# A fused retention and channel-mixing kernel: the order of the first loads, and the operand of the zero products

## The chip, the cores and the metric

The kernel runs on one core of one Trainium2 chip. The metric is the device time of one execution in microseconds (us), given as the median of several runs. A separate execution is taken by the hardware profiler; its span runs from the first to the last instruction on the core.

The engines are named as in the profile: PE is the matrix engine (TensorE; PEld its weight loads, which overlap with its products), DVE is VectorE, ACT is ScalarE, POOL is GpSimd, and SP is the engine that only issues transfers. ACT can issue transfers too. A trailing q (SPq, ACTq) stands for an issue.

## The reference

Two stages. The first is a retention layer over 4 batches, 8 heads, 768 positions and 64 channels, in blocks of 64 positions with a state that decays by head. The second is a channel-mixing layer on its output. Cut to what matters:

```python
# retention, for each block of 64 positions
intra = einsum('bhic,bhjc->bhij', qb, kb) * Dmask        # Dmask: powers of lam[h]
out   = einsum('bhij,bhjd->bhid', intra, vb) + einsum('bhid,bhde->bhie', qb * lam_pow, kv_state)
kv_state = lam_block * kv_state + einsum('bhsd,bhse->bhde', kb * rev_pow, vb)

# channel mixing on x, the output with all heads side by side (512 channels)
xk = mu_k * x + (1 - mu_k) * x_prev                      # x_prev: x one position earlier
xr = mu_r * x + (1 - mu_r) * x_prev
k  = maximum(xk @ w_k, 0)                                # 512 -> 1024
y  = sigmoid(xr @ w_r) * (k * k @ w_v)
```

## The kernel before

The positions are cut into six tiles of 128 (two blocks of 64 each), the heads into four pairs. Each tile passes through scores, decay, values and states of the four pairs, then through mixing, and then through the three large products with w_r, w_k and w_v. Each of those is done in three passes over operands split into a high and a low part, on 128x512 tiles.

The order of all work is written out by hand in one long string, ORDER. Each token names a step and its indices. All engines follow program order in their own queues, and waits between engines are semaphores. The string begins with `Z10 L00 T0 L02 A00 T2 a00 k02 A02 B00 k00 Sk4 ...`.

What the change and the steps of the prediction touch, all in the first 30 us:

- `zeros` is a work tile that VectorE clears with a memset (line 146). It is viewed as bfloat16 and used by `keep_busy` (line 200). Z10 issues ten products on `zeros` into the unused PSUM tile `idle`; each has 128 stationary and 512 moving columns. They compute nothing that is read later.
- `smalls` (30 KB) holds the small constants: the decay factors and their helpers, mixing weights, masks. `eye` (64 KB) is a 128x128 identity. SP issued the first, ScalarE the second.
- From `smalls`, VectorE, ScalarE and POOL build powers of the decay factors (`pows`, `steps`, `PW`, `KD`) and the tile `rows`. T0 transposes `rows` on PE with `eye` into `table`, from which the decay table Dt is copied.
- `load_first` issues SP's loads of the first tile's q, k and v, `in`: two transfers of 1 MB for head pairs 0 and 2, and two pairs of 768 and 256 KB for head pairs 1 and 3. In between, `stage_part` issues the halves of w_k, w_r and w_v (`raw`).
- Each weight half is converted once: `conv_top` casts part of its bits (`top`; for the blocks Sk4 to Sk7 on POOL, which waits for the half's landing alone), `conv_bits` puts the rest beside it (`raw`), `conv_split` makes the high and low parts (`wk`).
- `mix_prev` and `mix` make the mixed inputs (`ts`). POOL copies the last column of each (`lastw`), and `split_x` makes `xh` and `xl`.

Hardware transfers take eight semaphore counters in turn, in an order that the scheduler sets. A transfer that takes a counter again waits on the issuing engine until the transfer that had it before has landed.

Of the kernel before, what the change touches and what calls it, by code (L numbers as in the profile page):

```python
# [7 lines left out]
F32 = mybir.dt.float32  # L8
# [28 lines left out]
def tile_retention_moe(  # L37
# [25 lines left out]
    tensor, vector, scalar, gpsimd, sync = (  # L63
        InOrder(tc, e) for e in (tc.nc.tensor, tc.nc.vector, tc.nc.scalar, tc.nc.gpsimd, tc.nc.sync))
# [3 lines left out]
    work = ctx.enter_context(tc.tile_pool(name="work", bufs=2))  # L68
# [60 lines left out]
            sync.dma_start(t[rows, e:e + 2].rearrange("p c o -> p (c o)"), qv[n - 1, hp, rows])  # L129

    smalls = tiny.tile([128, 52 + H], F32, name="smalls")
    sync.dma_start(smalls, small)
    eye = work.tile([128, 128], F32, tag="rt", name="eye", bufs=4)
    scalar.dma_start(eye, hot)
    lows, impulse, ecol, lrow, erow, prow, mus, pair, parity = (smalls[:, a:b] for a, b in (
# [6 lines left out]
    KD = tiny.tile([128, H], F32, name="KD")  # L142
    one = tiny.tile([128, 1], F32, name="one")
    gpsimd.memset(one, 0.0)
    zeros = work.tile([128, 512], F32, tag="kf", name="zeros")
    vector.memset(zeros, 0.0)
    vector.memset(steps8[:, 0:8], 0.0)
    tops = const.tile([128, 2, 1024, 2], U16, tag="top", name="top")
# [30 lines left out]
    idle = ps_m.tile([128, 512], F32, tag="m", name="idle")  # L179
# [18 lines left out]
    zeros = zeros.bitcast(mybir.dt.bfloat16)  # L198

    def keep_busy(count):  # L200

        for _ in range(count):
            tensor.matmul(idle, zeros[:, 0:128], zeros[:, 512:1024], start=True, stop=True)

    def split(hi, lo, x):
        scalar.copy(hi, x)
# [285 lines left out]
    for step in ORDER.split():  # L492
        if step[0] == "T":
            powers(step)
        elif step[0] == "Z":
            keep_busy(int(step[1:]))
        else:
            i, j = step[1], int(step[2])
            steps[step[0]](i if i in "rkv" else int(i), j)
# [91 lines left out]
```

## Time and profile before

| | before |
|---|---|
| median of 3 runs | 398.38 us (397.89 to 399.62) |
| profiled execution, whole | 398.97 us |
| its span | 397.2 us |
| PE busy | 389.0 us, 98% |
| DVE busy | 245.5 us, 62% |
| ACT busy | 201.7 us, 51% |
| POOL busy | 39.8 us, 10% |
| bytes moved | 42.58 MB |

The span is the profiled execution less what lies around it, 1.77 us. Products are pipelined and their ends are modelled, so a product's length in a row is more than the distance to the next one. The granted clock is a share of 2.4 GHz. Transfers have two times: that of the issue (a row with SPq or ACTq) and the one from issue to landing. Queue q1 holds what SP issued, q10 what ScalarE issued; a packet is one row of a transfer, or the small write that reports an engine's share as done.

### The profile page before, as it was taken

Reading aid. Unit: us, or ns where it says so; the run is one execution under the profiler, and the core shown is the slowest. Engines: PE = TensorE matmul, PEld = TensorE weight load, DVE = VectorE, ACT = ScalarE, POOL = GpSimd, SP = SyncE. Lnnn points to the kernel's source line nnn. Section 1 sums busy time; section 2 is a strip of 40 time slices with the busy share of each in tenths; the row PEclk is TensorE's granted clock in tenths of the full one; section 3 lists DMA queues with packets and bytes.
Section 4 is the critical chain, followed back from the end, with each engine's and each line's share of the span. In section 5 each row is a group of like instructions: output and inputs, shape, how many; then the busy total and the mean of one; then the engine's idle time right before and its main releaser. Section 6 shows DMA issues by size and latency. Waiting matters only on the chain.

```text
span 397.2 us, 8411 instructions
## 1 busy us (share of the span) xinstructions
PE 389.0 (98%) x3532; PEld 321.3 (81%) x3532; DVE 245.5 (62%) x392; ACT 201.7 (51%) x367; POOL 39.8 (10%) x104
## 2 busy tenths in 40 slices
PE   7989999999999999999999999999999999999996
PEld 4758887888888888888888888888888888888886
DVE  5797899789865465876656365865546844222411
ACT  4889998565866172365721456731266542132400
POOL 5375000110110010000100010120000000000000
PEclk9999999999999999999999999999999999999999
DMA  7998735566060073170621070250100001000002
GB/s 275 417 356 276 295 125 174 169 150 216 11 205 0 10 218 94 28 186 0 184 57 54 28 194 20 82 159 26 53 2 2 2 1 55 26 26 2 0 34 73
DMA packets 12886, 42.58 MB, mean 107 GB/s; under 512 B 1840, under 2 KB 2224, under 8 KB 12592
## 3 DMA queue, kind: packets, MB, share of 16 engines
q1 hardware_dynamic: 9104, 35.68, 28.3%
q10 hardware_dynamic: 3744, 6.36, 4.4%
q8 instruction: 28, 0.46, 0.5%
q14 instruction: 10, 0.08, 0.1%
HBM read 35.74 MB, written 6.29 MB: 106 GB/s over the span
## 4 chain that ended last, share of the span: by engine, by line
PE 92%; DVE 2%; issue 1%; POOL 0%; ACT 0%; POOLq 0%
PE vp L33 33%; PE kp L33 31%; PE rp L33 17%; PE xp L33 5%; PE sc L33 3%; PE u L33 3%; DVE xl L33 1%; DVE raw L33 0%; DVE wk L33 0%; DVE ts L33 0%; POOL top L33 0%; POOL lastw L33 0%; DVE rt L33 0%; ACT st L33 0%; POOL ts L33 0%
## 5 line engine op out<-in xcount | busy, mean ns | idle before, releaser
L33 PE MATMUL vp<-wv,k 128*128 128x512 f32 (+1 forms) x600 | 134.7, 382 | 0.0
L33 PEld LDWEIGHTS vp<-wv,k 128*128 128x128 f32 x600 | 108.8, 188 | 22.2 <-DVE wv L33 0.3
L33 PE MATMUL kp<-xh,wk 128*128 128x512 f32 x384 | 123.1, 391 | 0.0
L33 PEld LDWEIGHTS kp<-xh,wk 128*128 128x128 f32 x384 | 72.0, 188 | 15.7 <-DVE wk L33 0.5
L33 PE MATMUL kp<-xl,wk 128*128 128x512 f32 x192 | 74.9, 390 | 0.1
L33 PE MATMUL rp<-wr,xh 128*128 128x512 f32 x192 | 59.5, 391 | 0.0
L33 DVE TENSOR_TENSOR kf<-kf 128x512 f32<-128x512 f32 x40 | 27.3, 691 | 51.6 <-ACT kf L33 51.4
L33 ACT ACTIVATE kf<-kp 128x512 f32<-128x512 f32 x48 | 28.2, 595 | 54.6 <-PE kp L33 38.1
L33 DVE TENSOR_TENSOR xl<-ts,xh 128x512 fp32r<-128x512 f32 x48 | 33.3, 699 | 21.7 <-ACT xh L33 21.6
L33 ACT COPY qv<-st 64x256 f32<-64x256 f32 x80 | 32.4, 405 | 27.3 <-DVE st L33 23.3
L33 ACT CAST xh<-ts 128x512 fp32r<-128x512 f32 x48 | 29.4, 617 | 29.5 <-DVE rt L33 22.9
L33 PEld LDWEIGHTS kp<-xl,wk 128*128 128x128 f32 x192 | 36.0, 188 | 8.1 <-DVE xl L33 0.7
L33 PEld LDWEIGHTS rp<-wr,xh 128*128 128x128 f32 x192 | 35.8, 188 | 7.6
L33 DVE TENSOR_TENSOR rt<-vp,rt 128x512 f32<-128x512 f32 (+1 forms) x25 | 16.4, 666 | 38.4 <-PE vp L33 38.4
L33 PE MATMUL rp<-wr,xl 128*128 128x512 f32 x96 | 37.4, 390 | 0.0
L33 ACT ACTIVATE ts<-xp,omu 128x512 f32<-128x512 f32 x40 | 26.2, 688 | 17.5 <-PE xp L33 16.1
L33 DVE TENSOR_TENSOR mv<-qv,LP 64x256 f32<-64x256 f32 x80 | 33.6, 420 | 1.5
L33 DVE TENSOR_TENSOR mv<-sc,Dt 64x512 f32<-64x512 f32 (+1 forms) x48 | 32.6, 685 | 2.3 <-ACT in L33 1.4
L33 DVE SCALAR_TENSOR_TENSOR ts<-xp,smalls,ts 128x512 f32<-128x512 f32 x40 | 29.2, 746 | 7.4 <-ACT ts L33 7.1
L33 DVE TENSOR_TENSOR k<-kf,k 128x1024 fp32r<-128x1024 f32 x24 | 29.3, 1224 | 7.0 <-ACT k L33 6.7
L33 POOL COPY ts<-lastw 128x4 f32<-128x4 f32 x48 | 18.0, 378 | 134.9 <-DVE xl L33 134.9
L33 ACT ACTIVATE rt<-rp 128x512 f32<-128x512 f32 x24 | 13.9, 592 | 30.7 <-PE rp L33 30.7
(66 smaller groups left out, 299.0 us busy)
## 6 DMA issues: line engine op xcount, KB each, us to landing
qv<-qv SPq DMA_DIRECT2D x40, 256.0 KB, 6.3
kin<-kk SPq DMA_DIRECT2D x20, 512.0 KB, 5.3
out<-rt ACTq DMA_DIRECT2D x23, 256.0 KB, 2.0
raw<-w_v SPq DMA_DIRECT2D x4, 1023.8 KB, 6.8
in<-qvk SPq DMA_DIRECT2D x2, 1024.0 KB, 6.1
raw<-w_k SPq DMA_DIRECT2D x2, 1023.8 KB, 13.0
raw<-w_k SPq DMA_DIRECT2D x4, 511.8 KB, 12.7
raw<-w_r SPq DMA_DIRECT2D x4, 511.8 KB, 15.2
```

The lines of the kernel that those rows point to most:

```text
L33: return lambda *args, **kw: self.tc.keep_in_program_order(op(*args, **kw))
```

## The change

Three edits. The load of `smalls` is issued by ScalarE, ahead of that of `eye`, and no longer by SP. The tile `zeros` has 64 words per partition in place of 512, so the memset is shorter. The zero products take these 64 words (128 bfloat16 values) as the stationary operand and, read four times over through a dimension of step zero, as the moving one. There are ten products before and after, each with 512 moving columns.

```diff
     smalls = tiny.tile([128, 52 + H], F32, name="smalls")
-    sync.dma_start(smalls, small)
+    scalar.dma_start(smalls, small)
     eye = work.tile([128, 128], F32, tag="rt", name="eye", bufs=4)
     scalar.dma_start(eye, hot)
...
-    zeros = work.tile([128, 512], F32, tag="kf", name="zeros")
+    zeros = work.tile([128, 64], F32, tag="kf", name="zeros")
     vector.memset(zeros, 0.0)
...
-            tensor.matmul(idle, zeros[:, 0:128], zeros[:, 512:1024], start=True, stop=True)
+            tensor.matmul(idle.rearrange("p (o x) -> p o x", o=4), zeros, zeros.rearrange("p (o x) -> p o x", o=1).broadcast_to([128, 4, 128]), start=True, stop=True)
```

SP's queue from its start, before. DMAHW0 to DMAHW7 are the eight counters; a number behind a name tells tiles of one name apart (`in_152` and `in_166` are head pairs 0 and 2, `in_214` and `in_216` pairs 1 and 3).

```order
L33 DMA smalls_103<-small 128x60
L33 DMA in_152<-qvk0 128x2048
L33 DMA in_166<-qvk0 128x2048
L33 DMA raw_206<-w_k 128x2047
L33 DMA in_214<-qvk0 128x1536
L33 DMA in_216<-qvk0 128x1536
L33 DMA in_214<-qvk0 128x512
L33 DMA in_216<-qvk0 128x512 [waits DMAHW0_49]
L33 DMA raw_206<-w_k 128x2047 [waits DMAHW1_49]
L33 DMA raw_276<-w_k 128x2047 [waits DMAHW2_49]
L33 DMA raw_276<-w_k 128x2047 [waits DMAHW3_49]
```

The same queue in the changed kernel.

```order
L33 DMA in_152<-qvk0 128x2048
L33 DMA in_166<-qvk0 128x2048
L33 DMA raw_206<-w_k 128x2047
L33 DMA in_214<-qvk0 128x1536
L33 DMA in_216<-qvk0 128x1536
L33 DMA in_214<-qvk0 128x512
L33 DMA in_216<-qvk0 128x512 [waits DMAHW0_49]
L33 DMA raw_206<-w_k 128x2047 [waits DMAHW1_49]
L33 DMA raw_276<-w_k 128x2047 [waits DMAHW2_49]
L33 DMA raw_276<-w_k 128x2047 [waits DMAHW3_49]
```

Every load of SP moves up by one place. The waits read alike, but other transfers have the counters: before, DMAHW0 to 3 were those of `eye`, `smalls`, `in_152` and `in_166`; now they are those of `smalls`, `in_152`, `in_166` and `eye`. From DMAHW4 on nothing differs.

ScalarE's queue from its start, before.

```order
L33 DMA eye_105<-hot 128x128
L33 ACT_TABLE_LOAD
L33 ACTIVATE one_111<-one_111 128x1 [waits Pool_49]
L33 ACTIVATE smalls_103<-smalls_103,pows_107 128x2 [waits DMAHW1_49,DVE_49]
L33 ACTIVATE smalls_103<-smalls_103,pows_107 128x4 [waits DVE_49,Activation_49]
```

And in the changed kernel.

```order
L33 DMA smalls_103<-small 128x60
L33 DMA eye_105<-hot 128x128
L33 ACT_TABLE_LOAD
L33 ACTIVATE one_111<-one_111 128x1 [waits Pool_49]
L33 ACTIVATE smalls_103<-smalls_103,pows_107 128x2 [waits DMAHW0_49,DVE_49]
L33 ACTIVATE smalls_103<-smalls_103,pows_107 128x4 [waits DVE_49,Activation_49]
```

One issue stands ahead of `eye`, of the activation table's load and of the small activations. PE's and POOL's orders are unchanged, and VectorE's too but for the size of its first memset.

## Rows read from the trace of the kernel before

**Rows 1.** The page: one engine's busy time; the last chain's shares by engine.

```profile
PE 389.0 (98%) x3532; PEld 321.3 (81%) x3532; DVE 245.5 (62%) x392; ACT 201.7 (51%) x367; POOL 39.8 (10%) x104
...
PE 92%; DVE 2%; issue 1%; POOL 0%; ACT 0%; POOLq 0%
```

**Rows 2.** Table of stretches: start:end, length, busy PE, PEld, DVE, ACT, POOL, clock, DMA.

```profile
5.70:9.40 3.70, 2.85 (x27) 2.18 (x26) 2.38 (x5) 1.46 (x5) 1.34 (x4) 1.00 1.01 363
30.00:390.00 360.00, 359.73 (x3258) 299.83 (x3258) 220.83 (x347) 180.14 (x328) 23.37 (x75) 1.00 0.28 88
```

**Rows 3.** Timeline, 0 to 6 us: start, length, engine, operation, [idle before, releaser].

```profile
0.73 0.42 ACTq L33 DMA_DIRECT2D eye<-hot  x1
...
0.73 0.38 SPq L33 DMA_DIRECT2D smalls<-small  x1
...
0.91 0.48 DVE L33 MEMSET zeros<- 128x512 f32 x1 [0.91 <-PEq L583]
1.17 0.90 SPq L33 DMA_DIRECT2D in<-qvk  x2
1.18 1.28 ACT L33 ACT_TABLE_LOAD   x1 [1.18 <-PEq L583]
1.35 0.07 DVE L33 MEMSET steps<- 128x8 f32 x1
...
1.45 4.45 PE L33 MATMUL idle<-zeros 128*128 128x512 bf16 x10 [1.45 <-DVE zeros L33]
...
2.65 0.63 ACT L33 ACTIVATE smalls<-smalls,pows 128x2 f32<-128x2 f32 x2
...
4.28 0.30 DVE L33 TENSOR_TENSOR rows<-smalls 128x136 f32<-128x136 f32 x1
...
5.69 1.13 PE L33 MATMUL table<-eye,rows 128*128 128x128 f32 x8
```

**Rows 4.** Issues in 0.7 to 2.31 and at 4.8 us: count, size, us to landing.

```profile
eye<-hot ACTq DMA_DIRECT2D x1, 64.0 KB, 1.9
smalls<-small SPq DMA_DIRECT2D x1, 30.0 KB, 1.7
...
raw<-w_k SPq DMA_DIRECT2D x1, 511.8 KB, 13.5
```

**Rows 5.** Chain of waits that ends at 40 us: start, length, piece.

```profile
18.34 0.77 POOL top L33
...
19.28 0.61 POOL lastw L33
...
29.79 10.31 PE kp L33 x44
```

**Rows 6.** Timeline, 4 to 20 us: the five w_k issues, one activation.

```profile
4.80 8.05 SPq L33 DMA_DIRECT2D raw<-w_k  x5
...
18.19 0.72 ACT L33 ACTIVATE ts<-raw,omu 128x512 f32<-128x512 f32 x1
```

**Rows 7.** Transfers in 4 to 6 us, all engines.

```profile
DMA packets 118, 0.84 MB, mean 418 GB/s; under 512 B 16, under 2 KB 16, under 8 KB 16
```

**Rows 8.** Transfer rate in 2.3 to 6.2 us, in 40 slices of 0.0975 us.

```profile
GB/s 84 84 252 84 168 0 84 84 168 504 420 420 420 420 420 504 420 420 504 252 420 504 336 336 420 588 252 336 588 420 336 504 336 420 504 336 336 420 420 252
```

**Rows 9.** Outputs issued at 141.94 and 152.14; packets by queue in 143.21 to 146.31.

```profile
out<-rt ACTq DMA_DIRECT2D x1, 256.0 KB, 4.9
...
out<-rt ACTq DMA_DIRECT2D x1, 256.0 KB, 2.1
...
q1 hardware_dynamic: 175, 0.56, 67.6%
q10 hardware_dynamic: 144, 0.26, 23.5%
```

**Rows 10.** Groups: DVE with a repeated operand (0 to 12 us), and without.

```profile
L33 DVE TENSOR_TENSOR mv<-sc,Dt 128x512 f32<-128x512 f32 x4 | 2.6, 686 | 1.9 <-ACT in L33 1.4 <-ACT Dt L33 0.5
...
L33 DVE TENSOR_TENSOR kf<-kf 128x512 f32<-128x512 f32 x40 | 27.3, 691 | 51.6 <-ACT kf L33 51.4
```

## The prediction, made before the changed kernel ran

> **What bounds the kernel now.** I read the page's shares first. TensorE is busy 98% of the span, and the chain that ended last is 92% PE [rows 1]. The table of stretches then says where PE is not busy: between 30 and 390 us it works 359.73 of 360 us [rows 2], so nothing in that stretch can be gained, and a stage before it is worth what it shifts the start of that unbroken run. All the change touches lies in the first 6 us. The question is how much earlier or later the run from 29.79 us starts.
>
> Two paths lead there.
>
> *The stream of loads.* The chain of waits goes back from 29.79 through conversions to POOL's cast `top` of the w_k half block at 18.34 [rows 5]. That cast waits for nothing but the block's landing. The DMA was issued at 4.80 and landed 13.5 us later, at 18.30 [rows 4, 6]. Its own 512 KB need 524 KB/418 GB/s = 1.25 us at the rate of the stretch 4 to 6 us [rows 7]; most of the rest it was queued behind earlier loads. So this landing moves with the start of the stream and not with its own issue.
>
> *The head.* The zero products start at 1.45, when the memset has ended at 0.91 + 0.48 = 1.39, and the table's transposes start at 5.69 behind them [rows 3]. The ten take 4.24 us, 0.424 each. Everything up to ScalarE's `ts` at 18.19 to 18.91 follows from there; POOL's `lastw`, which wants it, starts at 19.28 behind the cast [rows 5, 6]. So the head has 19.28 - 18.91 = 0.37 us of slack against the loads.
>
> **The change part by part.**
>
> *The memset.* 512 words took 0.48, the 8 of `steps` 0.07 [rows 3]. In a straight line between them 64 words take 0.07 + 0.41 x 56/504 = 0.12, so the zero products can start 0.36 us earlier, at 1.09, and end at 5.33 if each still takes 0.424. Without the fixed part (0.48 x 64/512 = 0.06) it would be 0.42.
>
> *The products that read 128 values four times.* Ten in number, as before, with as many columns. No row has a TensorE product whose moving operand repeats. The nearest are VectorE's: `mv<-sc,Dt`, which reads one head's table four times over, takes 686 ns for 512 columns, and the plain `kf<-kf` 691 [rows 10]. So repetition cost nothing there, and I put it at nothing here. A gain I exclude, as the same 512 columns pass; the other bound is twice the time, 4.24 us (below).
>
> *The first inputs at the head of SP's queue.* SP issued `smalls` at 0.73 and the first `in` at 1.17 [rows 3]; without the former the whole stream is issued 0.44 us earlier. What it loses: 30 and 64 KB of `smalls` and `eye` [rows 4] moved before the big rows had got going. The rate in 2.3 to 6.2 us stays under 260 GB/s for its first nine slices of 0.0975 us, up to 3.2 us, and is about 420 from there [rows 8]. If these 94 KB now fall into the full stream, they take 96 KB/418 GB/s = 0.23 us of it. So the stream moves by -0.44 to -0.21. I take -0.3, about the middle.
>
> *SP's waits.* A DMA waits for the one that last used its counter (the order in the section on the change). The second half of w_k's first block now waits for the first `in` rather than `smalls`: issued at about 5.8 instead of 4.80. The block behind it waits for the second `in`, and the next for `eye`. All of it is hidden: before the change that half landed 13.5 us after its issue, nearly all of it queueing, so one microsecond less of queueing is no later landing. If the queue ran dry it would cost that 1.0 us.
>
> *ScalarE.* One more issue before the activation table's load, 0.38 us: the load moves from 1.18 to 1.56 and ends at 2.84; the two small activations at 2.65 [rows 3] move to about 3.1 and end at 3.7. VectorE's `rows` at 4.28 wants them: hidden, with 0.6 us left.
>
> *The small transfers among the big rows.* `smalls` is issued at 0.73 still and landed 1.7 us later; `eye` goes from 0.73 to about 1.13, and with its 1.9 us lands at 3.03 if undisturbed [rows 3, 4]. But both now share the 16 engines with `in`. What that does is seen late in the kernel. An output of 256 KB, 128 rows, landed 2.1 us after its issue when alone, and 4.9 beside SP's loads; in that stretch SP's queue moved 175 packets and ScalarE's 144 [rows 9]. So rows of the two queues went about one for one, and the 8 rows that each engine had cost 2.8 us. An 8 KB row of `in` takes about 16 x 2.0/(118 - 16) = 0.31 us of an engine [rows 7], eight of them 2.5.
>
> For `smalls` I take nothing: it took 1.7 us with its landing, and the big rows reached their full rate only 3.2 - 1.17 = 2.0 us after their issue [rows 3, 8], now at 2.7 us. The far bound is +2.5 to +2.8. `rows` ended at 4.58, which leaves 5.33 - 4.58 = 0.75 us for a delay of `smalls`. For `eye`, half way through when the stream fills up, I take somewhere between 0 and 2.8: it lands between 3.0 and 5.8. The transposes then start between 5.33 and 5.85, which against 5.69 is -0.36 to +0.16; less the slack of 0.37 the head is ahead of the loads either way.
>
> The Trainium skill's page "DMA: Bandwidth & Descriptors", section "Issuing engines are not separate DMA queues", says that transfers of the different issuers run on the same 16 engines and interleave, and that a second issuer only saves the sequencer's time to start them. The trace agrees as to the mixing (175 and 144 packets in one stretch). By the page the whole gain is the saved issue, and the sum would be -0.44; by the row of the disturbed output the small transfers pay for it as well.
>
> **The sum.** Loads -0.3, head at most +0.16 - 0.37 = -0.21: the later of the two counts, between -0.2 and -0.3; I take -0.3. The profiled execution took 398.97 us (span 397.2), which becomes 398.7. It lies 0.6 above the median 398.38 of the runs shown, so that I forecast 398.1.
>
> **The rivals.**
>
> *Both small transfers are caught (slower).* If `smalls` has big rows before it on every engine, its 8 rows and then `eye`'s 8 go through one for one: 16 x 0.31 = 5.0 us on top of 3.03, so `eye` lands at 8.0 (2 x 2.8 by the output's row: 8.6). The transposes start 2.3 to 2.9 us later than 5.69; less 0.37 of slack the end comes 1.9 to 2.5 later: 400.3 to 400.9. It decides from a start of the transposes later than 5.69 + 0.37 = 6.06; below that it costs nothing. For it: the one-for-one mixing in [rows 9]. Against it: the 2.0 us that `in` needed to get going.
>
> *The stream does not start earlier*, because not SP's issue but the first rows themselves hold it up. The slow first slices in [rows 8] speak for it. Then the loads stay, the head hides behind them, and the time is 398.4.
>
> *The repeated operand is read more slowly.* At twice the time the zero products end at 1.09 + 8.48 = 9.57; +3.9 at the transposes, less 0.37: 401.9. For it speaks only that no row shows such a product; [rows 10] speak against.
>
> *TensorE's clock rises later.* The zero products take 0.424 us for 512 columns, the pace of 1.2 GHz, the lower of its two levels; for 5.7 to 9.4 us the granted clock is 1.00, 2.4 GHz [rows 2, 3]. If the zero products end early and PE then waits for `eye`, the rise could come after that stretch. Its 2.85 us of PE work [rows 2] would take twice that: +2.85 - 0.37 = +2.5, 400.9. Against it: the wait in my forecast is 0.5 us at most, behind 4.2 us of products. The Trainium skill's page "TensorE: Matmul & The Clock Gate", section "Part 1: The HAM clock gate", says that the moment of the rise isn't tied to the kernel's start and so varies from run to run; no row here shows that, and it would only scatter both kernels.
>
> **How the numbers follow.** The forecast has 0.64, the unchanged stream 0.13, the caught transfers 0.15 (a third of it over +2.0 us), the slower reading 0.03, the clock 0.03; 0.02 is left for what I don't see. A measurement of this kernel can tell about 0.5% from no change, 2.0 us. No term reaches that downward: faster 0.02. Slower: 0.05 + 0.03 + 0.03 less what falls short, 0.08. Same: 0.90. The runs of before lie between 397.89 and 399.62, so the scatter is wider than the forecast's own bounds; the range is 397.2 (the full -0.44 at a low median) to 400.0 (most of the caught transfers' partial cases).
>
> **What would show it.** Right: `in` issued first on SP at 0.73, zero products from about 1.09 with 0.42 us each, transposes between 5.3 and 5.9, POOL's cast of the w_k half near 18.0 and the unbroken run of PE from about 29.5. Wrong: `smalls` landing after 3.2, transposes after 6.06, zero products longer than 0.43 us apart, or the cast at 18.3 as before.

## The result, and the profile after

The changed kernel is slower: 402.74 us (median of 6 runs, 402.30 to 404.47) against 398.79 for the kernel before in the same comparison. The ratio is 1.0108, with an interval of 1.0088 to 1.0129. (Here and below the ratio is not the quotient of the two medians: it is worked out from all runs of both kernels.) The forecast was 398.1, with a range up to 400.0, so the time lies outside it. The mechanism stands in the prediction as its first rival, priced too low and given a chance of 0.15.

The profiled execution took 402.76 us, its span 401.0 against 397.2. The page's shares hardly moved, which is what one expects of a loss in the first 5% of a span:

```profile
PE 390.9 (97%) x3532; PEld 322.6 (80%) x3532; DVE 245.1 (61%) x392; ACT 201.5 (50%) x367; POOL 39.3 (10%) x104
...
PE 91%; DVE 2%; issue 0%; ACT 0%; DVEq 0%
```

The same stretch as in [rows 2] is as full as it was, so nothing was lost for lack of work after 30 us:

```profile
30.00:390.00 360.00, 359.95 (x3251) 299.36 (x3250) 224.92 (x353) 184.22 (x333) 25.39 (x76) 1.00 0.29 87
```

The timeline of the first microseconds, beside [rows 3] (start, length, engine, operation, idle time before and its releaser):

```profile
0.73 0.85 SPq L33 DMA_DIRECT2D in<-qvk  x2
0.74 0.41 ACTq L33 DMA_DIRECT2D smalls<-small  x1
...
0.82 0.11 DVE L33 MEMSET zeros<- 128x64 f32 x1 [0.82 <-PEq L583]
...
0.99 4.45 PE L33 MATMUL idle<-zeros 128*128 128x512 bf16 x10 [0.99 <-DVE zeros L33]
...
1.18 0.45 ACTq L33 DMA_DIRECT2D eye<-hot  x1
...
6.26 0.16 DVE L33 TENSOR_TENSOR pows<-smalls 128x1 f32<-128x1 f32 x1 [4.24 <-DMA smalls<-small]
...
8.09 0.30 DVE L33 TENSOR_TENSOR rows<-smalls 128x136 f32<-128x136 f32 x1
...
9.07 1.94 PE L33 MATMUL table<-eye,rows 128*128 128x128 f32 x8 [3.64 <-DMA eye<-hot]
...
10.94 2.08 PE L33 MATMUL sc<-in 64*128 64x128 f32 x16
...
14.52 1.16 PE L33 MATMUL sc<-in 64*128 64x128 f32 x16 [0.72 <-PE table L33]
```

The zero products are early, at 0.99 instead of 1.45, and take the same 4.45 us. Then PE stands idle for 3.64 us until `eye` is there. VectorE waited 4.24 us for `smalls`. The time from issue to landing, beside [rows 4], tells why:

```profile
smalls<-small ACTq DMA_DIRECT2D x1, 30.0 KB, 5.5
...
eye<-hot ACTq DMA_DIRECT2D x1, 64.0 KB, 7.8
```

1.7 us became 5.5, and 1.9 became 7.8. In the stretch 2.78 to 5.70 us the packets of the two queues (q1 SP's, q10 ScalarE's) are one for one, and nearly all bytes are SP's. The same holds in a stretch of half a microsecond, 6.0 to 6.5 us (the second pair of lines):

```profile
q1 hardware_dynamic: 152, 1.12, 91.8%
q10 hardware_dynamic: 153, 0.04, 7.3%
...
q1 hardware_dynamic: 26, 0.21, 100.4%
q10 hardware_dynamic: 26, 0.01, 8.8%
```

Cut finer, each of the eight quarters of a microsecond from 3.0 to 5.0 has 7 to 14 packets of SP and 7 to 15 of ScalarE, and in none do the two differ by more than two. So neither queue passes in bursts.

Nor did the start of the two loads come free. Between 0.5 and 2.9 us SP's queue had 21 rows under way, ScalarE's only 7, none of them before 2.7; the rate (40 slices of 0.06 us) rises at 1.7 us, is zero again from 1.9, and comes back after 2.4:

```profile
GB/s 0 0 0 0 0 0 0 0 0 0 0 0 0 0 0 0 0 0 0 0 410 546 137 0 0 0 0 0 0 0 0 0 273 683 0 137 0 4 137 570
...
q1 hardware_dynamic: 21, 0.17, 33.0%
q10 hardware_dynamic: 7, 0.00, 2.0%
```

The chain of waits no longer leads back to the cast of the w_k half, as it did in [rows 5]. The run of PE starts 4.07 us later than 29.79, behind ScalarE's and VectorE's work on the mixed inputs:

```profile
23.39 0.63 ACT ts L33
...
24.12 0.47 DVE ts L33
...
33.86 11.22 PE kp L33 x48
```

So the head sets the end now, and how it adds up can be read off four points. The second scores stood at 9.41 before:

```profile
9.41 1.16 PE L33 MATMUL sc<-in 64*128 64x128 f32 x16 [0.86 <-DVE mv L33]
```

From 5.69 to 9.07 the transposes are 3.38 us late. From 9.41 to 14.52 the second scores are 5.11 late: the 1.73 in between come from products at half the pace (1.94 us for the eight transposes instead of 1.13, 2.08 for the first scores where the second take 1.16). The table of stretches doesn't show this lower pace as a lower clock; its last columns are clock, DMA and GB/s:

```profile
9.00:13.80 4.80, 4.73 (x26) 3.80 (x26) 1.76 (x5) 0.65 (x2) 1.67 (x3) 1.00 0.99 381
```

The column reads 1.00 here, but it also reads 1.00 while the zero products pass at 0.42 us for 512 columns, the pace of 1.2 GHz, before and after the change; so in this trace it doesn't tell the two levels apart. The other five executions of the changed kernel show a mean granted clock of 0.987 to 0.991 (1.000 for the profiled one). That PE's clock was at the lower of its two levels is therefore read from the products' lengths, and the kernel with one edit alone, below, shows the clock itself. From 29.79 to 33.86 the run of PE is 4.07 late, so 1.04 was slack. The span is 3.8 longer: before the change PE waited once more after 30 us, for 0.3 us.

### The profile page after: what moved, and what is told of

It reads as the page before. It is cut to its first block, busy times and chain, and to the rows that moved or that the text cites. A ratio compares the mean times of both kernels' runs of the same rounds, so it can differ in the third digit from the quotient of the medians.

```text
span 401.0 us, 8411 instructions
## 1 busy us (share of the span) xinstructions
PE 390.9 (97%) x3532; PEld 322.6 (80%) x3532; DVE 245.1 (61%) x392; ACT 201.5 (50%) x367; POOL 39.3 (10%) x104
## 4 chain that ended last, share of the span: by engine, by line
PE 91%; DVE 2%; issue 0%; ACT 0%; DVEq 0%
PE vp L33 33%; PE kp L33 31%; PE rp L33 16%; PE xp L33 5%; PE sc L33 3%; PE u L33 2%; DVE xl L33 1%; DVE raw L33 0%; DVE ts L33 0%; DVE wk L33 0%; ACT ts L33 0%; ACT raw L33 0%; DVE rt L33 0%; ACT st L33 0%; DVEq L33 0%
```

## The experiments

The theory after the result, called *turns*: a row of a small load waits on each engine for one row of whatever big load stands in the other queue, and two small loads on one queue wait in series. The rivals: the loss comes from the product that reads 128 values four times, from the lower clock, from the bytes ahead and not from the rows, or from ScalarE's queue as such.

**One edit alone.** Only the move of `smalls`, on the kernel before:

```diff
-    sync.dma_start(smalls, small)
+    scalar.dma_start(smalls, small)
```

> The kernel before with one edit of the change: the load of smalls is issued by ScalarE ahead of eye; the zero products and their memset are the old ones. Theory (turns): the loss comes from the two small loads alone, whose rows go one for one with the 8 KB rows of SP's first loads on each of the 16 engines. Then smalls lands about 5.5 us after its issue, eye near 8.9, the transposes start near 9.0, and the time is 402.3 to 403.2. Rival (products): the loss comes from the product that reads 128 values four times, or from its shorter memset. Then this kernel has the time of before, 398.4 to 399.2, and the transposes start before 6.1.

Measured: 401.79 us against 398.34, ratio 1.0080 (1.0054 to 1.0106). `smalls` landed 5.5 us after its issue, `eye` 7.8, the transposes started at 9.06. So the loads alone make the loss, and the rival *products* falls. The time lies 0.5 us under what was expected, and the table of stretches shows where that comes from, and the clock itself:

```profile
6.40:9.80 3.40, 0.74 (x7) 0.77 (x8) 1.73 (x9) 0.59 (x2) 3.40 (x3) 1.00 0.98 346
9.80:13.20 3.40, 3.40 (x21) 2.41 (x19) 1.88 (x5) 0.65 (x2) 0.84 (x3) 0.50 1.03 419
13.20:20.00 6.80, 5.70 (x91) 4.87 (x92) 4.86 (x8) 5.85 (x12) 2.42 (x7) 1.00 1.03 417
```

The granted clock was 1.00 (2.4 GHz) in a stretch in which PE was busy for 0.74 of 3.40 us, then 0.50 (1.2 GHz) while it worked without a gap, then 1.00 again. The transposes began in the first stretch, at 9.06, and took 1.26 us; the first scores fell into the second and took 2.08. In the changed kernel both were slow.

**The other edit alone.** The short `zeros` and the repeated operand, with `smalls` on SP:

```diff
-    zeros = work.tile([128, 512], F32, tag="kf", name="zeros")
+    zeros = work.tile([128, 64], F32, tag="kf", name="zeros")
...
-            tensor.matmul(idle, zeros[:, 0:128], zeros[:, 512:1024], start=True, stop=True)
+            tensor.matmul(idle.rearrange("p (o x) -> p o x", o=4), zeros, zeros.rearrange("p (o x) -> p o x", o=1).broadcast_to([128, 4, 128]), start=True, stop=True)
```

> The other edit alone: zeros of 64 words, read four times, with smalls on SP as before. Theory (turns): smalls lands near 2.4 and eye near 2.6 as before; the zero products start at 1.0 and the transposes near 5.3, but the loads do not move, so that the time is 398.3 to 398.9, the same as before within 0.5 us. Rival (products): 402 or more, with the zero products further apart than 0.43 us or the rise of the clock late.

Measured: 398.96 against 398.34, ratio 1.0006 (0.9988 to 1.0025). No change, as expected. The zero products started at 0.99 and took 3.79 us (4.45 in the changed kernel), since the last of them already went at the higher pace; so the transposes started at 4.72, behind `rows`, and not near 5.3. The first scores then waited for `in`:

```profile
4.72 1.10 PE L33 MATMUL table<-eye,rows 128*128 128x128 f32 x8
6.09 1.16 PE L33 MATMUL sc<-in 64*128 64x128 f32 x16 [0.27 <-DMA in<-qvk]
```

The second scores still came 0.66 us early, at 8.75. Nothing came of it in this trace: PE then waited 2.0 us for ScalarE's `st` (1.5 before), and from 25 to 27 us the granted clock read 0.50, where the trace of before has 1.00.

**The clock's part.** The changed kernel with 22 zero products, which keep PE at work until `eye` lands:

```diff
-Z10 L00 T0 L02 A00 T2 a00
+Z22 L00 T0 L02 A00 T2 a00
```

> The changed kernel with 22 zero products in place of ten, so that PE works until about the landing of eye. Theory (turns, and a second part from the clock): the transposes still wait for eye until 8.8 to 9.3, but PE no longer stands idle before them and its clock is up: eight transposes in 1.1 us instead of 1.9, the first scores in 1.2 instead of 2.1. The time is 400.8 to 401.5, about half way back. Rival (no part for the clock, the delay of the loads is all): 402.5 to 403.0, as the changed kernel.

Measured: 401.71 against 398.34, ratio 1.0076 (1.0051 to 1.0101); 0.2 us above the theory's band and 0.8 under the rival's. The time alone doesn't show the clock's part: the kernel with the loads alone, which has ten zero products, measured 401.79 in the same comparison. The trace shows it up to the second scores:

```profile
8.92 1.06 PE L33 MATMUL table<-eye,rows 128*128 128x128 f32 x8 [0.49 <-DMA eye<-hot]
9.91 1.16 PE L33 MATMUL sc<-in 64*128 64x128 f32 x16
```

The second scores start at 12.57, 3.16 late instead of 5.11, and the run of PE at 31.91, 1.95 before that of the changed kernel. But the span is only 1.1 shorter, 399.9. What took the rest lies after 31.91, and no view shows it: the one wait there, 0.3 us that is put down to PE's own issue, the kernel before has too.

**The size of a row.** The changed kernel with SP's first two loads in halves, so that their rows are 4 KB:

```diff
-        sync.dma_start(first[hp][:, cuts[part]:cuts[part + 1]], qvk0[hp, :, cuts[part]:cuts[part + 1]])
+        step = 1024 if len(cuts) == 2 else 2048
+        for a in range(cuts[part], cuts[part + 1], step):
+            e = min(a + step, cuts[part + 1])
+            sync.dma_start(first[hp][:, a:e], qvk0[hp, :, a:e])
```

> The changed kernel with SP's first two loads of 1 MB each issued as two halves, so that their rows are 4 KB and not 8 KB. Theory (turns): a small row still waits for one big row, which is now half as long, about 0.16 us. Sixteen turns take 2.6 us instead of 5.0; smalls lands near 4.3, eye near 6, the transposes start at 5.8 to 6.4, and the time is 398.5 to 399.5. Rival (bytes): the small loads wait until the first loads' bytes have passed, whatever their rows; then smalls lands near 6.2, eye near 8.9, and the time stays at 402.3 to 403.2.

and with `step = 512`, rows of 2 KB:

> As the kernel with half rows, but the first two loads issued as four quarters each, so that their rows are 2 KB. Theory (turns): between the landing of smalls and that of eye lie the 8 turns of eye's rows, 2.7 us beside rows of 8 KB and 1.4 us beside 4 KB; here 0.6 to 0.9. From the issue of smalls to its landing there is a part that does not follow the row, the engines' first big rows: 5.5 and 4.6 us so far, here 3.6 to 4.3, and the transposes start at 6.2 to 7.0. Rival (bytes or a fixed delay of ScalarE's queue): the distance of the two landings stays at 1.2 us or more. The time is less telling, since SP's later loads now wait for smalls: 398.5 to 401.0.

Measured: halves 400.89 against 398.34, ratio 1.0061 (1.0039 to 1.0082); quarters 400.00 against 398.44, ratio 1.0043 (1.0016 to 1.0069). The halves measured 399.14 to 402.74, the quarters 398.45 to 401.96; the traces are of executions of 399.14 and 398.71, near the lower ends, and nothing shows what the others lose. The median of the halves lies between both theories, and so do its two landings, 5.3 for `smalls` and 6.8 for `eye`. What tells them apart is the distance between the landings. For halves, then quarters:

```profile
smalls<-small ACTq DMA_DIRECT2D x1, 30.0 KB, 4.6
eye<-hot ACTq DMA_DIRECT2D x1, 64.0 KB, 5.6
```

```profile
eye<-hot ACTq DMA_DIRECT2D x1, 64.0 KB, 4.4
smalls<-small ACTq DMA_DIRECT2D x1, 30.0 KB, 3.8
```

The issues are at 0.74 and 1.18 in the changed kernel, and 0.44 to 0.45 us apart in all three. `eye` lands 2.7 us after `smalls` beside rows of 8 KB (1.18 + 7.8 - 0.74 - 5.5), 1.4 beside 4 KB, and 1.0 beside 2 KB. So the wait gets shorter with the row, as *turns* has it and *bytes* doesn't: the bytes are the same. But the split also makes each load smaller and spreads the issues of SP's first two loads, from 0.73 to 2.85 us with halves instead of 0.73 to 1.58. The landings would shrink likewise if a turn were an engine's whole share of a load. That a turn is a single row is read from the even mixing of the packets above. The distance does not go to zero with the row: for 2 KB I had expected 0.6 to 0.9, and *bytes* 1.2 or more. `smalls` has a larger part that does not follow the row: from 5.5 to 4.6 to 3.8 where 1.7 is undisturbed. About 1.0 us of it in the changed kernel is the time up to 2.7 us in which only SP's rows moved, with the pause of 1.9 to 2.4 us in the rate above. Now `rows` came last, not `eye`, and the transposes started at 7.54 and 6.69.

**The place in the queues.** `eye` at the head of SP's queue, ahead of `in`, and `smalls` alone on ScalarE:

```diff
-    scalar.dma_start(eye, hot)
+    sync.dma_start(eye, hot)
```

> The changed kernel with eye moved to the head of SP's queue, ahead of the first inputs; ScalarE issues smalls alone. Theory (turns): a small load is caught only by big rows that are in the engines before it; now both small loads are issued at 0.73 and the first big rows come as late as before the change, so smalls lands by 2.6, eye by 2.8, the transposes start at 4.7 to 5.4, and the time is that of before within 1.0 us, 398.0 to 399.3. Rival (queue): a load that is issued by ScalarE waits behind SP's whatever stands there; then smalls lands after 4, the transposes start after 6.5, and the time is over 400.0.

Measured: 398.51 against 398.86, ratio 1.0005 (0.9988 to 1.0022). `smalls` landed 2.2 us after its issue, 0.3 later than expected, and `eye` 2.0 (2.0 and 2.2 in the kernel with the late head below, whose loads are those of before); the transposes started at 5.23:

```profile
smalls<-small ACTq DMA_DIRECT2D x1, 30.0 KB, 2.2
...
5.23 1.90 PE L33 MATMUL table<-eye,rows 128*128 128x128 f32 x8
```

This is still a load that ScalarE issues at 0.74. It is not the queue that makes it late, but big rows that are in the engines at the same time. The rival *queue* falls. The early start of the transposes bought nothing: they took 1.90 us instead of 1.13, at the lower pace of the zero products right ahead of them, and the second scores came 0.30 late. With the same start of the zero products, at 0.99, the higher pace came before the transposes in the kernel with the products alone, and only behind or within them here and in the kernel with the w_k half moved up, below (1.51 us).

The two issues on ScalarE in the other order:

```diff
-    scalar.dma_start(smalls, small)
     scalar.dma_start(eye, hot)
+    scalar.dma_start(smalls, small)
```

> The changed kernel with the two issues on ScalarE in the other order, eye and then smalls. Theory (turns): the two take their turns in the order of issue, so eye lands near 6.3 and smalls near 8.9, each with some 8 turns; what VectorE makes of smalls (1.9 us from its landing to the end of rows) then stands behind that, and the transposes start at 10.6 to 11.2. The time is 1.3 to 2.2 us above the changed kernel: 404.0 to 405.0. Rival (size: a small load is slow by itself beside the big ones, whatever its place): smalls lands near 6.3 again, eye near 8.9 or earlier, and the time stays at 402.3 to 403.2.

Measured: 404.51 (2 runs) against 398.86, ratio 1.0148 (1.0125 to 1.0171). `eye` landed 5.3 us after its issue and `smalls` 7.6, in the order of issue, and the transposes started at 10.96. All as expected of *turns*.

**The head alone.** The kernel before with 25 zero products (`Z25` for `Z10`), all loads as before:

> The kernel before with 25 zero products in place of ten and nothing else: the transposes start near 8.9 with the clock up, and all loads land as before. Theory (what counts is when the transposes start, not what holds them up): 2.6 to 3.6 us above before, 401.0 to 402.0, as the changed kernel with 22 zero products. Rival (the crowded loads themselves cost time further on, in the stream): less than that, 398.5 to 400.5, and the rest of the loss is in the stream.

Measured: 402.73 against 398.86, ratio 1.0107 (1.0088 to 1.0127): above both bands. The transposes started at 8.88 with the clock up, and the run of PE at 31.83, 2.04 late, as in the kernel with 22 zero products. So a late start of the transposes is enough, without a crowded load. But the span is 3.3 longer, 1.3 more than that. Behind 80 us PE has two waits put down to its own issue, 1.1 us together, where the kernel before has one of 0.3:

```profile
PE xp L33 <- issue: 0.6, 1, 0.6
PE kp L33 <- issue: 0.5, 1, 0.5
```

So some 0.8 of the 1.3 us is seen as waits. Whether the longer program makes them was not tried, and the time of this kernel is in part that of these waits.

**The landing that headed the chain.** The edit of the products, with the issue of the w_k half of [rows 5] ahead of two smaller loads of `in`:

```diff
-L01 L03 M01 Ck4 e00 B02 M03 A01 Sk5 A03
+L01 L03 Sk5 M01 Ck4 e00 B02 M03 A01 A03
```

> The kernel before with the short zeros tile and the repeated operand, and with the issue of the second half of w_k's first block moved ahead of the two 256 KB loads of pairs 1 and 3. Theory of the prediction (from 18.3 on the landing of that half is what the unbroken run waits for): it lands at 16.0 to 17.0 instead of 18.3, the head is 0.4 to 0.9 us earlier with its products, and the time is 397.4 to 398.2. Rival (the loads that are moved back are wanted as early): the activations on the keys of pairs 1 and 3 wait for them after 16, and the time is 398.3 to 399.5.

Measured: 399.42 against 398.86, ratio 1.0006 (0.9989 to 1.0023): no gain. The trace of before puts the start of this cast down to ScalarE's `st`, which ended at 18.29, just as the half landed. With the half ahead the cast started at 16.04, and `st` ended only at 20.26; so it was the landing that held the cast. But the run of PE started at 30.73, 0.94 later than before. The cast before, and in this kernel:

```profile
18.34 0.77 POOL L33 CAST top<-raw 128x512 f16<-128x512 bf16 x1 [3.21 <-ACT st L33]
...
16.04 0.89 POOL L33 CAST top<-raw 128x512 f16<-128x512 bf16 x1 [0.99 <-DMA raw<-w_k]
```

ScalarE had waited for the loads that were moved back (its waits in 10 to 24 us), and PE for ScalarE (0.7 us before):

```profile
PE xp L33 <- ACT raw L33: 2.4, 2, 1.7
...
ACT in L33 <- DMA in<-qvk: 1.8, 2, 1.0
```

The rival holds.

Side by side, from the traces (start of the transposes, of the second scores and of the unbroken run of PE, and the span; in brackets how late against before):

| kernel | transposes | second scores | run of PE | span |
|---|---|---|---|---|
| before | 5.69 | 9.41 | 29.79 | 397.2 |
| changed | 9.07 (+3.38) | 14.52 (+5.11) | 33.86 (+4.07) | 401.0 |
| loads alone | 9.06 (+3.37) | 13.82 (+4.41) | 33.17 (+3.38) | 400.0 |
| 22 zero products | 8.92 (+3.23) | 12.57 (+3.16) | 31.91 (+2.12) | 399.9 |
| half rows | 7.54 (+1.85) | 11.23 (+1.82) | 30.57 (+0.78) | 397.4 |
| quarter rows | 6.69 (+1.00) | 10.37 (+0.96) | 30.22 (+0.43) | 396.9 |
| late head | 8.88 (+3.19) | 12.50 (+3.09) | 31.83 (+2.04) | 400.5 |
| queues swapped | 5.23 (-0.46) | 9.71 (+0.30) | 29.59 (-0.20) | 396.4 |
| eye first | 10.96 (+5.27) | 16.43 (+7.02) | 35.78 (+5.99) | 402.7 |
| w_k half earlier | 5.23 (-0.46) | 9.32 (-0.09) | 30.73 (+0.94) | 397.8 |

The kernel with the other edit alone is left out: with the lower clock in between, its run starts at another product. In the kernels with quarter rows and swapped queues the cast of the w_k half sets the run again (it starts at 18.43 and 17.78), in the others whose transposes are late the head does. Each row is one execution, and the run itself took 366.7 to 368.7 us, so a span tells less than the starts.

## Why the prediction was wrong

**What bounds the kernel: right.** The unbroken run of PE kept its length within 0.3 us (401.0 - 33.86 = 367.1 against 367.4), and what changed was its start. The 0.3 is the wait of before named above.

**The memset and the repeated operand: right in their terms, without a measured effect.** The memset took 0.11 (forecast 0.12). The zero products started at 0.99 (1.09) and kept their length of 4.45 us. The one edit alone measured 1.0006. What the earlier end of the zero products gave was lost again further on: to the lower pace of the transposes in the kernel with the queues swapped, to a longer wait and a lower clock in that with the products alone.

**SP's stream: of no account.** The w_k half was issued at 6.62, later than the 5.8 that I worked out, because the `in` ahead of it in SP's queue now waited 2.4 us for `smalls`. It landed 10.3 us after that, at 16.9, 1.4 us earlier than before and not 0.3; why so much was not followed up:

```profile
raw<-w_k SPq DMA_DIRECT2D x1, 511.8 KB, 10.3
```

So the later issue was hidden. But that landing no longer set anything.

**ScalarE's extra issue: right.** The activation table's load moved to 1.66, and nothing waited for it.

**The small transfers: here it failed.** The step reads "For `smalls` I take nothing", on the ground that the big rows come to their full rate late. A low rate was taken for free engines. In the changed kernel the rate is near zero between 1.9 and 2.4 us, but 16 of SP's rows, as many as there are engines, had moved by 2.7 and none of ScalarE's. That an engine which has taken up a big row serves no other meanwhile would fit, and that the part shrinks with shorter rows (5.5, 4.6, 3.8); but no run showed a single engine, so what held `smalls` until 2.7 stays open. The loss of the two loads is shown (1.7 to 5.5, 1.9 to 7.8, with this edit alone), and so are the turns behind 2.7. The far bounds stood there, +2.5 to +2.8 for `smalls`, and were short too: it was +3.8, about 1.0 us up to 2.7 and the turns behind it.

**The rival's price.** For both caught I had worked out a start of the transposes 2.3 to 2.9 late; it was 3.38. From there the sum had two more wrong terms. The slack was put at 0.37, from the gap between ScalarE's `ts` and POOL's `lastw`; the table shows 1.04 (5.11 - 4.07), and the same within 0.01 in all kernels whose transposes start after 7.5. The `lastw` at 19.28 was the wrong one. POOL's order is unchanged, and in the changed kernel the copy that waits for this `ts` (23.29 to 24.01) is the next `lastw`, which stands at 20.07 before the change. The two paths meet at VectorE's step on `ts` beside it, which waited for POOL before and for ScalarE after:

```profile
20.05 0.76 DVE L33 SCALAR_TENSOR_TENSOR ts<-raw,smalls,ts 128x512 f32<-128x512 f32 x1 [0.21 <-POOL ts L33]
...
24.12 0.76 DVE L33 SCALAR_TENSOR_TENSOR ts<-raw,smalls,ts 128x512 f32<-128x512 f32 x1 [0.17 <-ACT ts L33]
24.14 0.19 POOL L33 COPY lastw<-ts 128x4 f32<-128x4 f32 x1 [2.23 <-ACT ts L33]
```

From the end of ScalarE's `ts` to this step it was 20.05 - 18.91 = 1.14 us before and 0.11 after. The 1.03 between them is the slack, and the step is 4.07 late, as the run of PE is. And the clock was priced as a rival of its own, with a chance of 0.03, against which I held that PE would wait 0.5 us at most. It is no independent case: PE waited 3.64 us because the loads were late, and behind that wait the products ran at the lower pace. It cost 1.73 on PE's way to the second scores. With PE kept at work by 22 zero products just that is gone (12.57 - 8.92 = 3.65 us between the two starts, 3.72 before, 5.45 after). Together: 3.38 + 1.73 - 1.04 - 0.3 further on = 3.8.

**The chances.** 0.15 for the rival was too little. [rows 9] already showed one-for-one turns and a price of 2.8 us; the only argument against was the slow start of `in`, and the trace of before could not show what occupies an engine in it.

The Trainium skill's page "DMA: Bandwidth & Descriptors", section "Queues, rings and completion order", says that each engine goes round its queues and takes a whole packet, typically some 9 to 17 descriptors, from one before it turns to the next. As to the going round, the trace agrees. As to the size of a turn it doesn't: with 8 rows of a small load on each engine, its whole share would pass in one turn, in a burst, and here the two queues' rows were mixed evenly down to quarters of a microsecond. The turn that fits is one row.

## What to carry to other kernels

A small load that early work waits for must be in the engines before the first big rows, whichever engine issues it: beside a big load with rows of 8 KB it waited about one big row for each of its own, and small loads on one queue add up. If the wait leaves PE idle for some microseconds, as here for 3.64, the lower pace of the products behind it belongs to the price of the wait (1.73 here). Slack is to be taken from where two chains meet, in the order that they would have if one were late, and not from a gap between two operations in the order that they have now.

## What the runs showed of the hardware

- The wait for big rows went with their size but not in proportion: `eye` landed 2.7, 1.4 and 1.0 us after `smalls` beside rows of 8, 4 and 2 KB.
- A load of 30 KB landed 1.7 us after its issue ahead of the big rows and 5.5 beside them, at the same time of issue; the 64 KB of `eye` went from 1.9 to 7.8.
- A TensorE product that reads 128 values four times over keeps the pace of one that reads 512: ten took 4.45 us either way.
- The higher pace of the products came at different times in traces whose zero products all started at 0.99: ten of them took 3.79 us in one kernel, and in two others the transposes behind the ten, from 5.23, still took 1.90 and 1.51 us instead of 1.13.
- With 25 zero products PE had waits of 0.6 and 0.5 us on its own issue later on; with 22 it had one of 0.3, as the kernel before has with ten. Their cause stays open.
